# A planned one-core kernel of chunked attention and a gated convolution layer: a new order of all steps, new choices of engines, another rule for filler matmuls

## The chip, the cores and the metric

The kernel runs on one core of a Trainium2 chip. The metric is the device time of one execution in microseconds. A run is one execution; the time before is the median of three.

## What is computed

```python
scores = scale * np.matmul(q_c, k_c.transpose(0, 1, 2, 4, 3))   # chunks of 64 rows, 8 x 8 x 9 of them
scores = scores - np.max(scores, axis=-1, keepdims=True)
attn = np.exp(scores)
attn = attn / (np.sum(attn, axis=-1, keepdims=True) + 1e-09)
out = np.matmul(attn, v_c)                                      # B, H, S, D = 8, 8, 576, 64
x = np.ascontiguousarray(attn_out.transpose(0, 2, 1, 3)).reshape(B, S, H * D)
...
h = np.maximum(x @ w_in, 0.0)                                   # 512 -> 1024
for k in range(K):                                              # 3 taps along the sequence
    conv_out += conv_w[k][None, None, :] * hp[:, k:k + S, :]
gate = 1.0 / (1.0 + np.exp(-conv_out))
return (h * gate @ w_out).astype(np.float32)                    # 1024 -> 512
```

The three weights arrive as 64-bit floats. The kernel reads them as pairs of 32-bit words and turns each into a high and a low part itself.

## The kernel before

**Tiles.** The 4608 rows of q, k and v are 36 tiles of 128 rows (two chunks of 64), numbered t0 to t35. Tiles t0 to t8 load their rows straight into one of three slots (`load_rows`, lines 126 and 133) and TensorE (PE) transposes them (`t_pe`, lines 196 and 201); t9 and later come by way of DRAM (`shuffle`, line 151; `load_part`, line 169) and VectorE (DVE) transposes them (line 217). Then come the scores (line 247, 32 matmuls), the maximum (line 257), the difference (261), the exponential on ScalarE (ACT, line 266), the sum (270), the small value added to it (274 or 276), the reciprocal (279) and the normalisation (line 319, on GpSimd, POOL, or DVE). PE transposes the probabilities (line 326), ACT or DVE copies them (lines 76 and 78), and `attn_v` multiplies them with the values (line 339, 32 matmuls). `x_hi` (ACT, line 394) and `x_lo` (DVE, line 398) put the result as two parts into the input of the next layer. From t12 on two tiles share a step `both` (the scores of two tiles and the values' product of the two before them; twelve such steps have scores), and their probabilities go through `s_fold`, `s_scale` and `p_swap`: two passes on POOL or DVE, then four small DMAs of SyncE's queue (line 313), then a transpose on DVE.

**First product.** The 4608 columns are twelve units u of 384. A block `mm1` (line 408) is one unit and one of eight groups of 128 features: 12 matmuls. Behind it ACT and DVE apply the rectifier (416, 418), the taps (446, 451), the tanh (462) and the gate (481).

**Second product.** It works on pairs of row tiles with seven products of 12 matmuls (`product`, line 512) in place of eight. Its factors are made from the gated values: a cast (lines 76, 78), a remainder (499), sums and differences (502). `product` needs all parts of w_out.

**Weights.** w_in is loaded in six pieces (two halves each of its first two quarters, then two quarters), w_out in four, conv_w in one, through `w_load` (line 544), into two places `w0` and `w1`. Each piece is taken apart: a scaled copy on ACT (558), a shift (562) and a word step (567) on DVE, a cast to the high part (76, 78), the remainder (571). For w_out the sums of Strassen's scheme come after the word step: differences on POOL (589 to 591), low parts (584 and 597). The piece of w_out loaded last is its second one. conv_w has small steps of its own on DVE (601 to 635). When the last word step and the last transpose of direct rows are done (`slot_users`), the memory of the slots is given to the ring of later tiles and to the factors of the second product.

**The order.** Nothing above runs in the order of the program text. Each call of `step` (line 80) notes an operation with an engine, a length and what it must follow; there are 1873, numbered in the order of the calls. `moved_` (line 963) puts some on another of their engines: entry x moves step x // 4 to its choice x % 4. `order_` (line 991) lists all steps. A loop goes through it, gives each step the earliest start that its engine, its predecessors and its buffers allow in a simple model of the machine, and hands out buffers. Then (line 1136) the steps are emitted by planned start, and a fixed order on each engine is kept. All DMAs are issued from SyncE's queue (SP) in that order, and one that has to wait holds those behind it.

**Fillers.** Up to a planned 110 us, line 1140 puts transposes of the identity matrix into planned gaps of PE:

```python
pe_free, until_ = 2.0, 110.0
...
            for _ in range(int((begin[i] - pe_free) / 0.14) if idle else 0):
                nc.tensor.transpose(out=banks[idle[-1]][:, 0:P], in_=ident, identity=ident)
            pe_free = begin[i] + steps[i]["cost"]
```

## Time and profile before

| | us |
|---|---|
| median of 3 runs | 478.6 (476.5 to 479.18) |
| the profiled execution | 477.3 |
| its span, from the first to the last instruction | 475.5 |
| PE, DVE, ACT, POOL busy | 464.0, 413.0, 257.7, 289.4 |
| first block of line 408 starts | 39.75 |
| first product of line 512 starts | 87.46 |

The page's busy shares are means over the span. Matmuls are pipelined and their ends are modelled, so PE can be busy throughout a stretch in which it does little, and a filler counts as busy like any other matmul. The order of time and the stretches tell the stages apart.

### The profile page before, as it was taken

Reading aid. Unit: us, or ns where it says so; the run is one execution under the profiler, and the core shown is the slowest. Engines: PE = TensorE matmul, PEld = TensorE weight load, DVE = VectorE, ACT = ScalarE, POOL = GpSimd, SP = SyncE. Lnnn points to the kernel's source line nnn. Section 1 sums busy time; section 2 is a strip of 40 time slices with the busy share of each in tenths; the row PEclk is TensorE's granted clock in tenths of the full one; section 3 lists DMA queues with packets and bytes.
Section 4 is the critical chain, followed back from the end, with each engine's and each line's share of the span. In section 5 each row is a group of like instructions: output and inputs, shape, how many; then the busy total and the mean of one; then the engine's idle time right before and its main releaser. Section 6 shows DMA issues by size and latency. Waiting matters only on the chain.

```text
span 475.5 us, 13438 instructions
## 1 busy us (share of the span) xinstructions
PE 464.0 (98%) x5481; PEld 452.9 (95%) x5481; DVE 413.0 (87%) x775; ACT 257.7 (54%) x535; POOL 289.4 (61%) x260
## 2 busy tenths in 40 slices
PE   8989889999999999999999999999999999999996
PEld 8879889999999999999999999999999999999996
DVE  2869999999999898989988999898998998788694
ACT  2557989955555463554564465453545545444631
POOL 0124678976777666767667857467868553633523
PEclk9989999999999999999999999999999999999999
DMA  6878999998789999999938283600361100101002
GB/s 195 237 216 255 282 207 193 188 162 205 133 143 211 200 204 160 157 228 165 221 80 149 60 208 80 166 23 23 102 167 45 46 23 2 46 1 68 8 38 112
DMA packets 186369, 64.33 MB, mean 135 GB/s; under 512 B 159660, under 2 KB 177092, under 8 KB 186308
## 3 DMA queue, kind: packets, MB, share of 16 engines
q1 hardware_dynamic: 186308, 63.48, 61.9%
q8 instruction: 43, 0.70, 0.6%
q14 instruction: 18, 0.15, 0.1%
HBM read 50.88 MB, written 23.59 MB: 157 GB/s over the span
## 4 chain that ended last, share of the span: by engine, by line
PE 89%; DVE 5%; ACT 2%; issue 2%; POOL 1%; POOLq 0%; DVEq 0%
PE b_ps L512 38%; PE b_ps L408 38%; PE sx_ps L247 3%; PE sx_ps L339 3%; PE b_ps L196 2%; PE b_ps L1140 2%; PE z_ps L339 1%; DVE wt L567 1%; PE z_ps L247 1%; PE b_ps L326 1%; DVE gt L451 1%; DVE wt L562 1%; DVE m L257 1%; ACT wt L558 0%; DVE wt L261 0%
## 5 line engine op out<-in xcount | busy, mean ns | idle before, releaser
L512 PE MATMUL b_ps<-wo_h,f 128*128 128x256 f32 x1008 | 190.6, 282 | 0.1
L512 PEld LDWEIGHTS b_ps<-wo_h,f 128*128 128x128 f32 x1008 | 158.6, 188 | 2.2 <-POOL f L78 0.7
L512 PE MATMUL b_ps<-wo_l,f 128*128 128x256 f32 x504 | 141.3, 280 | 0.6 <-issue 0.6
L451 DVE SCALAR_TENSOR_TENSOR gt<-b_ps,cw,gt 128x384 f32<-128x384 f32 (+3 forms) x208 | 116.6, 576 | 9.0 <-ACT gt L446 7.1
L499 POOL TENSOR_TENSOR f<-gt,f 128x512 fp32r<-128x512 f32 x71 | 91.8, 1298 | 29.3 <-ACT f L76 9.8
L512 PEld LDWEIGHTS b_ps<-wo_l,f 128*128 128x128 f32 x504 | 94.9, 188 | 0.3 <-issue 0.3
L408 PE MATMUL b_ps<-x_h,wi_h 128*128 128x386 f32 (+2 forms) x384 | 84.7, 342 | 0.9 <-DVE gb L481 0.9
L408 PE MATMUL b_ps<-x_l,wi_h 128*128 128x386 f32 (+2 forms) x384 | 83.3, 338 | 0.0
L408 PE MATMUL b_ps<-x_h,wi_l 128*128 128x386 f32 (+2 forms) x384 | 83.1, 338 | 0.0
L462 ACT ACTIVATE gt<-gt 128x384 f32<-128x384 f32 (+2 forms) x96 | 50.2, 523 | 43.8 <-DVE gt L451 43.6
L408 PEld LDWEIGHTS b_ps<-x_l,wi_h 128*128 128x128 f32 x384 | 68.8, 188 | 0.0
L408 PEld LDWEIGHTS b_ps<-x_h,wi_l 128*128 128x128 f32 x384 | 68.6, 188 | 0.0
L408 PEld LDWEIGHTS b_ps<-x_h,wi_h 128*128 128x128 f32 x384 | 65.7, 188 | 1.8 <-DVE gb L481 1.2
L446 ACT ACTIVATE gt<-b_ps,cw 128x384 f32<-128x384 f32 (+2 forms) x104 | 56.4, 555 | 18.0 <-DVE b_ps L418 16.3
L416 ACT ACTIVATE b_ps<-b_ps 128x386 f32<-128x386 f32 (+2 forms) x78 | 37.3, 479 | 51.5 <-PE b_ps L408 47.6
L502 POOL TENSOR_TENSOR gt<-gt 128x512 f32<-128x512 f32 x43 | 55.5, 1295 | 15.2 <-PE b_ps L408 6.0
L481 DVE SCALAR_TENSOR_TENSOR gt<-gt,b_ps 128x192 f32<-128x192 f32 (+2 forms) x120 | 47.2, 410 | 8.1 <-ACT gt L462 7.4
L78 POOL CAST f<-gt 128x512 fp32r<-128x512 f32 x42 | 25.8, 613 | 33.9 <-PE b_ps L512 24.1
L76 ACT CAST f<-gt 128x512 fp32r<-128x512 f32 x43 | 26.5, 617 | 25.2 <-PE b_ps L512 14.8
L217 DVE STREAM_TRANSPOSE qkT<-qk 128x1024 f32<-128x1024 f32 (+1 forms) x30 | 33.3, 1119 | 0.4 <-DMA qk<-rows 0.4
L524 ACT ACTIVATE wt<-b_ps 128x256 f32<-128x256 f32 x50 | 18.9, 381 | 24.9 <-PE b_ps L512 24.9
L499 POOL TENSOR_TENSOR f<-gb,f 128x512 fp32r<-128x512 f32 x14 | 18.1, 1294 | 17.8 <-ACT f L76 8.7
(96 smaller groups left out, 614.8 us busy)
## 6 DMA issues: line engine op xcount, KB each, us to landing
out<-wt SPq DMA_DIRECT2D x36, 256.0 KB, 3.7
qk<-rows SPq DMA_DIRECT2D x24, 320.0 KB, 5.0
rows<-in_k SPq DMA_DIRECT2D x12, 576.0 KB, 8.7
rows<-in_q SPq DMA_DIRECT2D x12, 576.0 KB, 8.3
qk<-rows SPq DMA_DIRECT2D x24, 256.0 KB, 4.5
v<-in_v SPq DMA_DIRECT2D x21, 256.0 KB, 5.0
w<-in_moe_w_out SPq DMA_DIRECT2D x4, 1024.0 KB, 6.1
wt<-wt SPq DMA_DIRECT2D x48, 64.0 KB, 2.0
```

The costliest lines, as they stand in the source:

```text
L76: nc.scalar.copy(out=out, in_=in_)
L78: ENG[eng].tensor_copy(out=out, in_=in_)
L217: nc.vector.transpose(out=to[:, :, i:i + n], in_=of[:, :, o:o + n])
L408: nc.tensor.matmul(h_ps[:, 0:w], lhsT=wt[:, f // 2, kt, P * (f % 2):P * (f % 2) + P], rhs=xt[:, u % NX, kt, 0:w], start=n == 0, stop=n == ...
L416: nc.scalar.activation(out=h, in_=h, func=AF.Relu)
L446: nc.scalar.mul(out=g, in_=h, mul=cw[:, FT + f:FT + f + 1])
L451: nc.vector.scalar_tensor_tensor(out=g, in0=h, scalar=w, in1=g, op0=ALU.mult, op1=ALU.add)
L462: nc.scalar.activation(out=g, in_=g, func=AF.Tanh, scale=0.5)
L481: nc.vector.scalar_tensor_tensor(out=o, in0=g, scalar=1.0, in1=hv, op0=ALU.add, op1=ALU.mult)
L499: ENG[eng].tensor_tensor(out=part(st, 1), in0=quarter(*src), in1=part(st, 0).bitcast(F32), op=ALU.subtract)
L502: ENG[eng].tensor_tensor(out=quarter(*out_), in0=quarter(*a), in1=quarter(*b), op=op)
L512: nc.tensor.matmul(o, lhsT=part(ft, a)[:, j, :], rhs=w[:, i, j, :], start=first and n == 0, stop=n == 3 * FT // 2 - 1, skip_group_check=True)
```

## The change

The diff touches what a reader can put into four groups.

1. Options that are set to nothing: `PLAIN = 0` (a second product without Strassen's scheme for the first pairs), `TAPS = 0` (the convolution's taps as matmuls for the first units), `HOMED = ()` (rows loaded into the place of the gated values). Their functions and branches are in the text and emit nothing. The step numbers stay the same, 0 to 1872.
2. The model of loads: other lengths (`lag`), a limit of eight outstanding DMAs in the queue, a limit on how far the queue runs ahead (`ahead`), and a count of DMAs in a step (`m`). They act on planned starts alone.
3. Both lists, `moved_` (197 entries before, 194 after, 80 in both) and `order_`, are new.
4. The rule for fillers.

```diff
-            ld = step("SP", 1.2 if (2 * t) % NCK < NCK - 1 else 2.3, load_key, load_rows, (st, t), take=[(r, st)], lag=1.9 if t < NP else 2.8)
+            cost = 1.2 if (2 * t) % NCK < NCK - 1 else 2.3
+            ld = step("SP", cost, load_key, load_rows, (st, t), take=[] if t in HOMED else [(r, st)], lag=(2.35 if cost < 2 else 2.9) if t < NP else 3.0,
+                      ahead=1.7 if t < NP else 1.1, m=2 if cost < 2 else 4)
...
-    dma_free, kind, bank = 3.5, 0, {}
+    dma_free, ring_end, kind, bank = 1.6, {"SP": 0.0, "ACT": 0.0, "POOL": 0.0}, 0, {}
+    landed = {"SP": [0.0] * 8, "POOL": [0.0] * 8}
...
-        if e == "SP":
-            dma_free = max(dma_free, t + 0.3 + cost / 2) + s["lag"]
-            end[i] = max(dma_free + 1.5, t + cost + 2.0)
         free_at[e] = t + cost - early[e]
+        if s["lag"]:
+            ring, x = landed["SP" if e == "ACT" else e], t
+            for j in range(s["m"]):
+                x = max(x, ring[-8 + j]) + cost / s["m"]
+            free_at[e] = max(x, ring_end[e]) - early[e]
+            dma_free = max(dma_free, x - cost / 2 + 0.3) + s["lag"]
+            end[i] = max(dma_free + 1.5, x + 2.0)
+            ring += [end[i] - s["lag"] * (s["m"] - 1 - j) / s["m"] for j in range(s["m"])]
+            ring_end[e] = dma_free - s["ahead"]
...
-    pe_free, until_ = 2.0, 110.0
+    pe_free, until_ = 1.4, 110.0
...
-            for _ in range(int((begin[i] - pe_free) / 0.14) if idle else 0):
+            wait = begin[i] - pe_free - 0.3
+            for _ in range(int((wait + 0.3) / 0.164) if pe_free < 2.0 else int(wait / 0.115) + 1 if idle and wait > 0 else 0):
                 nc.tensor.transpose(out=banks[idle[-1]][:, 0:P], in_=ident, identity=ident)
```

What the numbers of the two lists mean, for the parts that the prediction speaks of (wi0a is the first half of the first quarter of w_in, wo1 the second piece of w_out, rows, v, and so on with their tile):

```
SP, before:  rows t0, cw, rows t1, rows t2, wi0b, rows t3, wi0a, v t0, rows t4, wi1a, rows t5, v t1, wi1b, wi3, v t2, ...
SP, after:   rows t0, rows t1, wi0a, cw, rows t2, v t0, rows t3, wi0b, rows t4, wi1a, v t1, wi1b, rows t5, v t2, wi3, ...
             (wo1 is the 27th load in both)

PE, before:  ... t_pe t3 (2), scores t2, p_pe t0, t_pe t4 (2), attn_v t0, p_pe t1, scores t3, t_pe t5, scores t4, attn_v t1, ...
             attn_v t2, p_pe t3, t_pe t6 (2), mm1 u0
PE, after:   ... scores t2, t_pe t3 (2), p_pe t0, attn_v t0, scores t3, t_pe t4, p_pe t1, t_pe t4, attn_v t1, p_pe t2, scores t4, ...
             attn_v t2, scores t5, p_pe t3, mm1 u0
   ahead of the first product, before alone: one mm1 block of u1; after alone: attn_v t7

DVE, after, of what stood ahead of the last word step (wo1) from the copy of t0's second half on:
   no longer there: copies of q and k of t1 (2) and t5, the normalisation of t4, the remainder of wi1a
   new there:       six steps of cw (they ran before that copy), the cast of wi0a, the remainder of wi0b, the copies of the
                    probabilities of t2 and t3, a copy of q and k of t6, the normalisations of t3 and t6, three small softmax steps
   of it ahead of the start of mm1 u0: all new ones but the copies of t3 and t6, the normalisation of t6 and two of the
                    small steps; and the shift and word step of wi3 and the maximum of t5 stand behind it now

POOL, before: ... differences wo2, low parts wo2 (2), differences wo1, f_sum, normalisation t7, low part wo1, last low part wo1
POOL, after:  ... differences wo2, low part wo2, differences wo1, low part wo1, last low part wo2, last low part wo1, f_sum
   of 12 s_fold and 12 s_scale: 9 and 12 on POOL before, 11 and 11 after; 241 steps on POOL before, 228 after
```

## Rows read from the trace of the kernel before

**Rows 1.** The page: busy time, share of the span and number of instructions of PE, PE's weight loads, DVE, ACT and POOL.

```profile
PE 464.0 (98%) x5481; PEld 452.9 (95%) x5481; DVE 413.0 (87%) x775; ACT 257.7 (54%) x535; POOL 289.4 (61%) x260
```

**Rows 2.** Busy time by stretch: the stretch and its length, then busy us of each engine (with the number of instructions), the granted PE clock, the DMA engines' busy share and GB/s.

```profile
9.57:24.73 15.16, 13.77 (x375) 11.82 (x376) 12.50 (x24) 6.75 (x13) 1.89 (x2) 1.00 0.82 221
24.73:28.70 3.97, 3.55 (x65) 2.98 (x65) 0.00 (x1) 2.63 (x6) 0.94 (x1) 0.58 0.66 181
28.70:39.75 11.05, 10.32 (x197) 9.49 (x196) 10.48 (x19) 6.71 (x15) 3.57 (x6) 1.00 0.82 249
39.75:87.46 47.71, 44.47 (x467) 42.31 (x464) 46.23 (x98) 43.52 (x89) 33.65 (x30) 1.00 1.07 234
...
39.75:87.46 47.71, 2.37 (x17) 1.76 (x15) 1.00 1.07 234
...
110.00:471.50 361.50, 360.74 (x3981) 356.59 (x3980) 321.34 (x579) 182.19 (x380) 230.32 (x201) 1.00 0.53 111
```

The shorter row for 39.75 to 87.46 is the same view of the fillers (line 1140) alone.

**Rows 3.** The waits of PE over the whole span: who waited for whom, us in total, times, the longest.

```profile
PE sx_ps L339 <- ACT p_all L76: 1.5, 1, 1.5
...
PE b_ps L408 <- DVE gb L481: 0.9, 1, 0.9
PE b_ps L512 <- issue: 0.6, 1, 0.6
```

**Rows 4.** The fillers (line 1140): duration in ns (least, median, most), first and last start; and the sum of their busy time over the seven stretches of 10 us that hold any, on PE and of the weight loads.

```profile
L1140 PE MATMUL b_ps<-ident x112: 271/273/472, 1.4 to 93.7; 128*128 128x128 f32 x112
...
sum 70.00, PE 18.43 PEld 14.63; mean PE 2.63 PEld 2.09
```

**Rows 5.** PE in order of time: start, us, line, operation, out<-in, count, and in brackets the idle time before it with its releaser.

```profile
1.36 5.73 PE L1140 MATMUL b_ps<-ident 128*128 128x128 f32 x35 [1.36 <-POOL ident masks.py:199]
7.02 1.16 PE L196 MATMUL b_ps<-ident,qk 128*64 128x64 f32 x32
...
25.15 0.88 PE L339 MATMUL sx_ps<-p_all,v 64*64 64x64 f32 x26 [1.81 <-issue]
...
27.43 1.13 PE L247 MATMUL sx_ps<-qkT 64*64 64x64 f32 x32
...
30.26 0.69 PE L247 MATMUL sx_ps<-qkT 64*64 64x64 f32 x32
...
39.75 0.95 PE L408 MATMUL b_ps<-x_h,wi_h 128*128 128x384 f32 x4
...
87.46 0.36 PE L512 MATMUL b_ps<-wo_h,f 128*128 128x256 f32 x1
```

**Rows 6.** The waits of DVE from 0 to 90 us, columns as in rows 3.

```profile
DVE m L257 <- PE sx_ps L247: 5.9, 3, 4.0
```

**Rows 7.** The waits of SP's queue over the whole span, columns as in rows 3.

```profile
SPq L313 <- POOL wt L307: 53.9, 8, 18.4
...
SPq L126 <- PE b_ps L196: 2.9, 1, 2.9
```

**Rows 8.** Line 126 between 0.6 and 2.2 us, its first two DMAs: duration of the issue, and the time from issue to landing.

```profile
L126 SPq DMA_DIRECT2D qk<-in_q x1: 767/767/767, 0.7 to 0.7; - x1
L126 SPq DMA_DIRECT2D qk<-in_k x1: 635/635/635, 1.6 to 1.6; - x1
...
DMA to landing us min/median/max: 3.3/3.4/3.4
```

**Rows 9.** The page's DMA queues (packets, MB, share of 16 engines' span) and its DMA issues (count, KB each, median us to landing).

```profile
q8 instruction: 43, 0.70, 0.6%
...
wt<-wt SPq DMA_DIRECT2D x48, 64.0 KB, 2.0
```

**Rows 10.** DVE and POOL in order of time, columns as in rows 5.

```profile
22.39 0.68 DVE L567 SCALAR_TENSOR_TENSOR wt<-w,wt 128x512 uint32<-128x512 uint32 x1
22.99 0.68 DVE L270 TENSOR_REDUCE z<-wt 128x8 f32<-128x512 f32 x1
...
72.38 2.05 DVE L567 SCALAR_TENSOR_TENSOR wt<-w,wt 128x1024 uint32<-128x1024 uint32 x1
...
74.57 2.39 POOL L597 TENSOR_TENSOR wo_l<-wt,wo_h 128x1024 fp32r<-128x1024 f32 x1 [1.23 <-ACT wt L266]
77.66 1.28 POOL L589 TENSOR_TENSOR wt<-wt 128x512 f32<-128x512 f32 x1 [0.69 <-DVE f L499]
...
79.84 0.74 POOL L591 TENSOR_TENSOR wt<-wt 128x256 f32<-128x256 f32 x1
...
82.79 2.02 POOL L584 TENSOR_TENSOR wo_l<-wt,wo_h 128x256 fp32r<-128x256 f32 x2
84.76 2.45 POOL L597 TENSOR_TENSOR wo_l<-wt,wo_h 128x1024 fp32r<-128x1024 f32 x1
```

**Rows 11.** Groups of instructions on DVE: out<-in, shapes, count | busy us, mean ns of one | idle us before them.

```profile
L78 DVE COPY qkT<-b_ps 128x512 f32<-128x512 f32 x5 | 3.3, 677 | 1.7 <-PE b_ps L196 1.7
...
L614 DVE SCALAR_TENSOR_TENSOR wt<-w,wt 24x128 f32<-24x128 uint32 x1 | 0.3, 278 | 0.0
L610 DVE TENSOR_SCALAR wt<-w 24x128 uint32<-24x128 uint32 x1 | 0.2, 207 | 0.0
```

**Rows 12.** The chain of work in order of time: start, us, what.

```profile
107.76 2.11 PE b_ps L408 x12
...
114.54 0.62 PE sx_ps L339 x32
```

More of the change, by code (lines that the diff above doesn't have):

```diff
@@ L58, in attn_ffn @@
     DIRECT = ()
+    PLAIN = 0
+    TAPS = 0
+    HOMED = ()
     scale = 1.0 / float(D) ** 0.5
@@ L71, in attn_ffn @@
     steps = []
-    ENG = {"DVE": nc.vector, "POOL": nc.gpsimd}
+    ENG = {"DVE": nc.vector, "POOL": nc.gpsimd, "SP": nc.sync, "ACT": nc.scalar}
     def copy_on(eng, out, in_):
@@ L78, in copy_on, with step @@
             ENG[eng].tensor_copy(out=out, in_=in_)
-    def step(eng, cost, key, fn, args=(), after=(), take=(), free=(), lag=0.0, port=False, bank=None, other=(), soft=()):
+    def step(eng, cost, key, fn, args=(), after=(), take=(), free=(), lag=0.0, port=False, bank=None, other=(), soft=(), ahead=1.1, m=1):
         s = dict(eng=eng, cost=cost, key=key, fn=fn, args=args, after=[a for a in after if a], take=take, free=free,
-                 lag=lag, port=port, bank=bank, other=other, soft=[a for a in soft if a])
+                 lag=lag, port=port, bank=bank, other=other, soft=[a for a in soft if a], ahead=ahead, m=m)
         steps.append(s)
@@ L678, in split_o @@
         st = {}
-        ld = step("SP", 0.55, t_load, w_load, (st, src_o[n]), take=[("wslot", st)], lag=3.5)
+        ld = step("SP", 0.55, t_load, w_load, (st, src_o[n]), take=[("wslot", st)], lag=3.5, ahead=5.0)
         s1 = step("ACT", 1.15, key, w_scale, (st,), [ld], take=["wt"])
@@ L819, in ring @@
                         shuffled[b, i] = [step("SP", 0.55, key - 20 + 0.1 * n, shuffle, (b, i, n), lag=4.0) for n in range(2)]
-                    got += [step("SP", 0.55, key + 0.1 * n, load_part, (c0, c1, i, n), slot_users + old + shuffled[b, i], lag=1.35) for n in range(2)]
+                    got += [step("SP", 0.55, key + 0.1 * n, load_part, (c0, c1, i, n), slot_users + old + shuffled[b, i], lag=1.45, ahead=3.0) for n in range(2)]
                 group_loads.update(dict.fromkeys(range(c0, c1), got))
@@ L888, in pair_steps, with mul, copy @@
         w_all = [x for n in range(FT // 2) for x in wo_done[n]]
-        def mul(name, i, key, bank_, half, first, after, take=()):
+        def mul(name, i, key, bank_, half, first, after, take=(), free=(("ft", "ft"),)):
             ft = fts[name]
             before["o"] = step("PE", 1.425, key, product, (st, ft, i, bank_, half, first), [ft["made"]] + w_all + after,
-                               take=list(take), free=[("ft", "ft")], soft=[before.get("o")])
+                               take=list(take), free=list(free), soft=[before.get("o")])
             return before["o"]
-        def copy(row, col, key, after, **kw):
-            return step("ACT", 0.39, key, o_copy, (st, row, col), after, other=[("DVE", 0.43, False)], **kw)
+        def copy(row, col, key, after, bank_="y", **kw):
+            return step("ACT", 0.39, key, o_copy, (st, row, col, bank_), after, other=[("DVE", 0.43, False)], **kw)
+        if p < PLAIN:
+            for row, b_ in enumerate("yq"):
+                at = key + 4 + 4 * d * row
+                one, two = f"A{row + 1}1", f"A{row + 1}2"
+                x = mul(one, 0, at, b_, 0, True, [], [("bk", st, b_)], [])
+                c = copy(row, 1, at, [x, before["st"] if row else None], b_, **({} if row else {"take": ["wt"]}))
+                if not row:
+                    before["st"] = c
+                x = mul(two, 1, at + d, b_, 0, False, [c], [], [])
+                c = copy(row, 0, at + d, [x, c], b_)
+                x = mul(one, 3, at + 2 * d, b_, 1, True, [c])
+                x = mul(two, 2, at + 3 * d, b_, 1, False, [x])
+                e = step("DVE", 0.43, at + 3 * d, o_last, (st, row, 1, b_), [x, c], free=[("bk", b_)])
+                last = step("SP", 0.5, key + 13 + row / 2, o_store, (st, 2 * p + row), [e, c] + ([last] if row else []),
+                            free=["wt"] if row else [], lag=0.65, ahead=5.0)
+            return
         p1 = mul("A11", 0, key + 4, "y", 0, True, [], [("bk", st, "y")])
@@ L927, in wi @@
             end for i, ks in enumerate(parts)
[L928 removed]
+            for end in split(key + 2 * i, t_load + 0.1 * i, src_i[n][:, ks], wi_h[:, n, ks, :], wi_l[:, n, ks, :], half=len(parts) > 1,
+                             at=None, **kw)]
     cw_done = split(8.0, 0.15, src_c)
@@ L953, in attn_ffn @@
             pair_steps(3 * (u - 1) // 2 + 2, PK[3 * (u - 1) // 2 + 2])
+    for s, f in home_next:
+        s["after"] += [home_users[i] for i in range(len(home_users)) if 1024 * i < 2 * UN * (f + 1) and 1024 * (i + 1) > 2 * UN * f]
     for s, over in x_writes:
```

133 lines of the change are left out of this document (89 added, 44 removed), and 212 rows, old and new, of tables (moved_, order_).

## The prediction

> **What bounds the kernel now.** I read the page first: TensorE (PE) is busy 98% of the span, VectorE (DVE) 87% [rows 1]. A share over the whole span hides stages, so the next view was busy time by stretch [rows 2]. From 110 to 471.5 us PE is busy 360.74 of 361.5 us, and of the waits that its list names only the "issue" of 0.6 us lies there [rows 3]: nothing is left to gain in that stage, whose matmuls are the same in both kernels. The last fourteen PE steps stand in the same order in both lists, so the end is the same too. So a gain has to come from before 110 us, where PE is "busy" partly with fillers: 112 of them cover 18.4 us [rows 4], and only 2.4 us of that lies between 39.75 and 87.46 [rows 2].
>
> What holds PE there? The first block of the first product (line 408) starts at 39.75 us, the first of the second (line 512) at 87.46 [rows 5]. Between them DVE is busy 46.23 of 47.71 us, ACT 43.52, PE 44.47 with fillers [rows 2]: this stretch is DVE's. Before it DVE loses time: 2.66 us in 9.57 to 24.73, and then 3.97 us in one piece (24.73 to 28.70), a wait for the scores of tile 3 [rows 2, 6]. The cause stands in PE's order of time: the attention product of tile 0 stopped after 6 of its 32 matmuls and went on with 26 at 25.15; the 1.81 us ahead of them are "issue", no wait that the profile shows. [...]
>
> The load queue (SP) has a hole as well: the rows of tile 3 wait 2.9 us for the slot that tile 0's transposes still read, and all loads behind them with it [rows 7].
>
> **The change part by part.** The new options (PLAIN, TAPS, HOMED) are zero or empty, so no new instruction runs. Live are the order, 194 engine choices (80 of the 197 old ones stay), the rule for fillers, and the plan's model of loads, which acts through the other three alone.
>
> *First fillers.* The old rule puts (6.94 - 2.0)/0.14 = 35 of them ahead of the first transposes; the row has 35, from 1.36 to 7.02, that is 0.162 us each [rows 5]. The two loads which those transposes read were issued at 0.7 and 1.6 us and landed 3.4 and 3.3 us later [rows 8], by 4.9: the fillers, not the data, held the start back. By the new lines of the loop (1.6 in place of 3.5 for the queue's start, lag 2.35 for 1.9) the planned start is 5.49, so (5.49 - 1.4)/0.164 = 24 fillers; these are counts that the code emits. 11 x 0.162 = 1.8 us, less 0.1 for a wait on the data: **-1.7** at the start of every chain; the slot comes free as much earlier. Bounds: 0 (data late) and -2.1 (7.02 - 4.9). Later fillers: planned gaps up to 0.3 us get none now (up to two before), gaps of 0.5 us two in place of three, gaps over 1 us the same or one more. One filler takes 0.27 us [rows 4], in a gap that mostly waits anyway; I take 0 and put -0.5 into the range.
>
> *The stall at 23 us.* In the new lists tile 0's values are loaded ahead of tile 3's rows, where the hole in the queue was, and on PE the scores of tile 3 come right behind the attention product of tile 0, with tile 4's transposes behind them in place of in front. DVE has weight work and softmax of tiles 1 and 2 to do ahead of those scores. If the stall goes, DVE keeps its 3.97 us; if it comes back at the same count of PE instructions, it hits the transposes of tile 4, which no engine needs soon. I take **-4.0**; bounds 0 (it returns on the path) and -4.0.
>
> The queue table has 43 packets of the instruction queue, 0.70 MB [rows 9], 16 KB each. [...]
>
> *DVE's work.* I counted, in both lists, the DVE steps from its copy of tile 0's second half (9.57 us) to the last weight piece's word step (line 567, ends at 74.43 [rows 10]); all factors of the second product wait for that one, since their buffers lie where the weight slots were. Out: three copies of q and k to ACT, a normalisation and a weight remainder to POOL, 5 steps of 0.68 us. In: six small steps on the convolution weights that ran ahead of 9.57 (1.48 us together), a weight cast, a remainder, two copies of probabilities, one of q and k, two normalisations (0.68 each), and 1.05 us of small softmax steps (one sum as long as a copy, a reciprocal, the small value added) [rows 11]. That is 7.29 - 3.40 = 3.9 us; consecutive DVE steps overlap by 0.08 us (22.39 + 0.68 against 22.99 [rows 10]), for 11 more steps 0.9: **+3.0** on the path. Its bounds are 0 (other work stands in PE's way) and +3.9. For the start of line 408 the same count gives 1.8 us less DVE work than before, so that start should come at 39.75 - 1.7 - 4.0 - 1.8 = 32.2, at the latest 36.
>
> *The chain behind it on POOL.* Before: word step done at 74.43, the difference on POOL from 77.66, then a sum and a normalisation, low parts of 2.02 and 2.45 us, end 87.21 [rows 10], product at 87.46 [rows 5]: 12.8 us on POOL's side. Now the difference comes ahead of the other piece's remainder (2.39), and sum and normalisation are behind it or on DVE: from 77.66 on without the two in between, that is 2.9 (77.66 to 80.58) + 2.0 + 2.4 + 2.45 = 9.8 us. **-3.0**; bounds -3.0 and 0 (if the shared order of DVE and POOL holds the difference back as before).
>
> *PE's order.* One block of line 408 (2.11 us) moved behind the first product, one attention product (0.62) ahead of it [rows 12]: **+1.5** still to do at that point. Changes between kinds of matmuls are as many, within two.
>
> *Everything later:* 0. Its covers are the 40 us that DVE and the 131 us that POOL are idle from 110 us on [rows 2]; if they fail, PE waits: third rival.
>
> **Sum:** -1.7 - 4.0 + 3.0 - 3.0 + 1.5 = -4.2 us at the first product, kept to the end since PE is full from there. The profiled execution took 477.3 us (span 475.5), so 473.1; the median of the runs is 1.3 higher, 478.6, so **474.4 us**, -0.9%. About 0.5% (2.4 us) is what a measurement of this kernel can tell from no change.
>
> **Rivals.** (1) The stall returns on the path: the -4.0 falls away, the sum is -0.2, **478.4 us**. For: the wait belongs to no data, and PE runs through as many instructions in the first 30 us as before. Against: the new order puts nothing urgent there. (2) DVE doesn't set the first product, PE's own work does. Then the start's gain is kept whole (1.7 + 4.0 + 1.8, less 0.9 for two transposes that moved behind it, 6.6), and of the 3.2 us of idle time and 2.4 us of fillers between 39.75 and 87.46 [rows 2] half goes too: -9.4, **469.2 us**. Against: DVE's 97% in that stretch. (3) Slower: the twelve combined steps of tiles 12 on wait for probabilities that pass POOL, four DMAs of 2.0 us to landing [rows 9] and DVE; SP, in order, already waits 53.9 us for POOL ahead of those DMAs, once 18.4 [rows 7]. The new lists give POOL 22 of their 24 folding and scaling passes in place of 21, and put stores and loads of values elsewhere in SP's order. From (4.2 + 2.4)/12 = 0.55 us of lateness at each step the kernel would be slower by over 0.5%; at 0.6 us it is +7.2 - 4.2, **481.6 us**. Against: that wait doesn't once reach PE now [rows 3], and POOL has 13 steps fewer. (4) Fewer fillers drop the clock. A fall like the one at 25 us costs half of its stretch of 4 us, so three among line 408's blocks would undo the gain and give again about 478. Idle pieces of 0.9 and 1.5 us [rows 3] left the clock at 1.00 from 28.70 on [rows 2], so this is counted inside (1).
>
> [...]
>
> **How the numbers follow.** Forecast 0.48, its own range 471.8 to 477.4 (-0.5 and -2.1 at the fillers on one side; POOL's 3.0 lost on the other). Rivals 1 and 4: 0.25; rival 2: 0.13; rival 3: 0.14. Faster by over 0.5%: the forecast without its upper edge, and rival 2: 0.60. Within 0.5%: rival 1 and that edge, 0.26. Slower: 0.14. The range 470.5 to 479.4 leaves out rival 3 and half of rival 2.
>
> **What would show it.** Right: first transposes at about 5.3 us behind some 24 fillers; no DVE wait near 4 us for the scores of tile 3; line 408 from 32 to 36 us; first product at about 82; the last remainder (line 597) ends right ahead of it. Wrong: an "issue" wait of over 1 us on PE with scores behind it (rival 1); PE waiting for POOL or DVE between 75 and 90 us (the -3.0); PE waiting for probabilities or x in the combined steps (rival 3); a granted clock under 1.00 after 35 us (rival 4).

## The result and the profile after

The changed kernel takes 482.58 us (median of 8 runs, 480.59 to 484.92), the kernel before 478.08 in the same session (8 runs, 476.5 to 483.43). The ratio is 1.0109 with a 95% interval of 1.0086 to 1.0132: slower by 1.1%, where 474.4 was forecast. The profiled execution took 480.59 us, 3.3 more than that of before, with a span of 478.8. Line numbers have moved: 408 is 414 now, 512 is 549, 247 is 253, 339 is 345, 196 is 202, 1140 is 1227. Runs with a disturbed clock are left out of all comparisons.

The page, answering [rows 1]. Every engine but ACT has less to do:

```profile
PE 463.4 (97%) x5477; PEld 452.5 (95%) x5477; DVE 409.3 (85%) x773; ACT 265.5 (55%) x550; POOL 277.4 (58%) x247
```

The waits of PE over the whole span, answering [rows 3]:

```profile
PE b_ps L549 <- issue: 2.0, 1, 2.0
PE sx_ps L345 <- ACT gt L483: 1.8, 1, 1.8
PE b_ps L207 <- DVE gb L518: 1.4, 1, 1.4
...
PE b_ps L202 <- DMA qk<-in_k: 1.2, 1, 1.2
...
PE z_ps L253 <- issue: 0.7, 1, 0.7
```

PE in order of time, answering [rows 5]:

```profile
1.36 4.58 PE L1227 MATMUL b_ps<-ident 128*128 128x128 f32 x24 [1.36 <-POOL ident masks.py:199]
5.86 2.10 PE L202 MATMUL b_ps<-ident,qk 128*64 128x64 f32 x64
...
9.43 1.16 PE L202 MATMUL b_ps<-ident,qk 128*64 128x64 f32 x32 [1.22 <-DMA qk<-in_k]
10.52 0.70 PE L253 MATMUL sx_ps<-qkT 64*64 64x64 f32 x32
...
21.99 0.69 PE L345 MATMUL sx_ps<-p_all,v 64*64 64x64 f32 x32
22.51 0.65 PE L253 MATMUL sx_ps<-qkT 64*64 64x64 f32 x32
...
35.93 0.94 PE L414 MATMUL b_ps<-x_h,wi_h 128*128 128x384 f32 x4
...
66.08 0.91 PE L345 MATMUL sx_ps<-p_all,v 64*64 64x64 f32 x32 [1.80 <-ACT gt L483]
...
69.92 0.96 PE L414 MATMUL b_ps<-x_h,wi_h 128*128 128x388 f32 x4
...
86.93 0.28 PE L549 MATMUL b_ps<-wo_h,f 128*128 128x256 f32 x1
...
162.74 1.16 PE L345 MATMUL sx_ps<-p_all,v 64*64 64x64 f32 x64
163.72 1.11 PE L253 MATMUL z_ps<-qkT 64*64 64x64 f32 x64
...
169.04 0.51 PE L549 MATMUL b_ps<-wo_h,f 128*128 128x256 f32 x2 [2.02 <-issue]
...
211.28 0.34 PE L253 MATMUL z_ps<-qkT 64*64 64x64 f32 x8 [0.68 <-issue]
```

A wait for "issue" is one for which the trace shows nothing that PE waited for; it is called an issue wait below, and unit 1 begins with the first matmul of 388 columns. Read from the top: 24 fillers, transposes at 5.86 (7.02 before). The attention product of tile 0 runs through at 21.99 and the scores of tile 3 follow at once: the stall of 23 us is gone. Line 414 starts 3.8 us earlier than line 408 did. But unit 1 (69.92 against 67.97) is 1.9 us later, the first product only 0.5 us earlier, and behind it two waits for "issue" come to 2.7 us where before had 0.6.

So 3.3 us are made up of -0.5 at the first product and +3.8 behind it (478.8 - 86.93 = 391.9 us, before 388.0). Of the 3.8, 1.5 are the PE order that the prediction counted and 2.1 the issue waits. The medians lie 4.5 us apart, 1.2 more than the profiles: the runs of after have a mean granted clock of 0.993 (0.988 to 0.996, the profiled one 0.996), 16 runs of before in the next session 0.9985. A straight line through after's eight runs gives 3.3 us more for each 0.01 of clock lost (correlation 0.81), so the clock would account for the 1.2; that is a fit, not an experiment.

### The profile page after: what moved, and what is told of

Read it like the earlier page. It is cut to its first block, busy times and chain, and to the rows that moved or that the text cites. A ratio compares the mean times of both kernels' runs of the same rounds, so it can differ in the third digit from the quotient of the medians.

```text
span 478.8 us, 13446 instructions
## 1 busy us (share of the span) xinstructions
PE 463.4 (97%) x5477; PEld 452.5 (95%) x5477; DVE 409.3 (85%) x773; ACT 265.5 (55%) x550; POOL 277.4 (58%) x247
## 4 chain that ended last, share of the span: by engine, by line
PE 88%; DVE 5%; DMA 2%; ACT 2%; issue 1%; POOL 1%; SPq 0%; ACTq 0%; POOLq 0%; DVEq 0%
PE b_ps L414 40%; PE b_ps L549 38%; PE sx_ps L345 2%; PE sx_ps L253 2%; PE z_ps L345 1%; DMA qk<-in_k 1%; PE b_ps L202 1%; PE z_ps L253 1%; DVE wt L605 1%; DMA w<-in_moe_w_in 1%; PE b_ps L1227 1%; ACT wt L596 1%; POOL wi_l L609 1%; DVE x_l L404 1%; PE b_ps L332 0%
## 5 line engine op out<-in xcount | busy, mean ns | idle before, releaser
L536 POOL TENSOR_TENSOR f<-gt,f 128x512 fp32r<-128x512 f32 x61 | 79.0, 1299 | 47.3 <-ACT f L79 22.1
L539 POOL TENSOR_TENSOR gt<-gt 128x512 f32<-128x512 f32 x41 | 52.9, 1293 | 11.2 <-DVE f L536 5.3
L79 ACT CAST f<-gt 128x512 fp32r<-128x512 f32 x50 | 30.8, 617 | 30.5 <-PE b_ps L549 26.0
L81 POOL CAST f<-gt 128x512 fp32r<-128x512 f32 x36 | 22.0, 612 | 35.7 <-PE b_ps L549 21.9
L561 ACT ACTIVATE wt<-b_ps 128x256 f32<-128x256 f32 x55 | 20.6, 381 | 22.3 <-PE b_ps L549 22.3
L536 POOL TENSOR_TENSOR f<-gb,f 128x512 fp32r<-128x512 f32 x18 | 23.3, 1294 | 16.5 <-ACT f L79 9.2
```

The costliest lines, as they stand in the source:

```text
L79: nc.scalar.copy(out=out, in_=in_)
L81: ENG[eng].tensor_copy(out=out, in_=in_)
L536: ENG[eng].tensor_tensor(out=part(st, 1), in0=quarter(*src), in1=part(st, 0).bitcast(F32), op=ALU.subtract)
L539: ENG[eng].tensor_tensor(out=quarter(*out_), in0=quarter(*a), in1=quarter(*b), op=op)
```

## Where the lead of 3.8 us goes

Busy time by stretch, columns as in [rows 2]: from the first scores to the first block of line 414 (408), and from there to the end of DVE's first piece of x_l of tile 6 (128x4), which unit 1's second four matmuls read. First after, then before, then e8, the old lists without the stall (below).

```profile
10.52:35.93 25.41, 24.16 (x608) 21.83 (x605) 21.37 (x47) 15.31 (x30) 4.47 (x5) 1.00 0.81 228
35.93:67.96 32.03, 26.84 (x329) 24.72 (x327) 30.40 (x55) 26.75 (x52) 17.97 (x18) 0.98 0.96 252
```

```profile
10.80:39.75 28.95, 26.41 (x607) 23.25 (x603) 22.11 (x41) 16.10 (x32) 6.40 (x8) 0.94 0.81 226
39.75:67.96 28.21, 25.45 (x330) 23.97 (x328) 27.07 (x49) 26.79 (x52) 16.48 (x15) 1.00 1.04 260
```

```profile
9.80:36.89 27.09, 24.96 (x607) 22.03 (x603) 22.18 (x41) 16.20 (x32) 6.61 (x8) 1.00 0.89 242
36.89:64.93 28.04, 25.75 (x331) 24.36 (x329) 26.57 (x49) 26.54 (x52) 16.21 (x14) 1.00 0.96 257
```

The third busy figure is DVE. Up to the first block after has 4.04 us of idle DVE (25.41 - 21.37), before 6.84, e8 4.91. In the second stretch after has 30.40 us of DVE work in 32.03, before 27.07 in 28.21: 3.3 us more, and the stretch is 3.8 us longer. It ends at 67.96 us in both kernels, so the lead of 3.8 us is gone there: the early start is owed work. After's unit 1 then begins another 1.95 us later than before's. e5 (below) has the same PE steps there, its x_l piece ends at 67.93, and its granted clock is 1.00 from 60 to 70 us, where after's is 0.83. First after, then e5:

```profile
66.92 1.11 PE L207 MATMUL b_ps<-ident,qk 128*128 128x128 f32 x4
67.83 2.34 PE L1227 MATMUL b_ps<-ident 128*128 128x128 f32 x11
```

```profile
66.68 0.66 PE L207 MATMUL b_ps<-ident,qk 128*128 128x128 f32 x4
67.17 1.36 PE L1232 MATMUL b_ps<-ident 128*128 128x128 f32 x11
68.29 0.95 PE L414 MATMUL b_ps<-x_h,wi_h 128*128 128x388 f32 x4
```

So in these two executions the clock costs after 1.6 us at unit 1 (69.92 against 68.29), of which 1.0 is in the eleven fillers that the new rule puts there (before has four). At the first product 0.8 is left (86.93 against 86.15).

## Experiments

A matmul takes two places in PE's program, itself and its weight load (the pages have as many of both, 5477 in after and 5481 in before), and each of the small matmuls below appears in the trace as two (e1's 73 as 146, e6's 40 as 80); the expectations count places, the text matmuls as the trace has them. Each kernel has 6 to 12 runs. Results are medians, with ratios to the kernel before in the same session (477.1 to 478.0 us) and their 95% intervals.

### Do the issue waits hang on the place in the program?

The expectations set two theories against each other. 'Blocks': an issue wait hangs on how many matmuls PE has run, so a shift takes it away or moves it. 'Place': it belongs to its time, whatever stands there, and stays. By 'blocks' e1 was expected at about 480 us, and e5, further below, at about 480.5 with under 1 us of issue waits behind 110 us.

**e1, e2.** In after and in before, nine of the first fillers become 73 small matmuls, so that everything behind stands 137 matmuls later.

```diff
-            for _ in range(<24 in after, 35 in before>):
+            for _ in range(73):
+                nc.tensor.matmul(banks[idle[-1]][0:64, 0:64], lhsT=ident[0:64, 0:64], rhs=ident[0:64, 0:64], start=True, stop=True)
+            for _ in range(<15, 26>):
```

> The changed kernel with 9 of its 24 first fillers replaced by 73 small ones (64x64), so that every later PE instruction stands 128 places further in PE's instruction stream. [...] Rival 'place': the waits belong to what else the chip does at 167 and 210 us, not to the count of instructions. Then they stay and the time is 482.6.

> The kernel before with the same shift of 128 places (9 of its 35 first fillers replaced by 73 small ones). Theory 'blocks': the issue wait of 0.6 us near 165 us goes, and the one of 1.8 us at 23 us (row 962 of PE's instructions) leaves the attention product of tile 0; without it the stretch to line 408 is up to 4 us shorter, of which PE's later order keeps up to 2. About 475.5 to 477.5 in place of 478.1. Rival 'place': both stay, 478.1.

Measured: 500.62 us (1.0483, 1.0433 to 1.0533) and 493.13 (1.0319, 1.0275 to 1.0363). The times tell nothing of the issue waits, since the small matmuls were slow:

```profile
1.36 15.83 PE L1228 MATMUL b_ps<-ident 64*64 64x64 f32 x146 [1.36 <-POOL ident masks.py:199]
```

What holds is that the waits changed: behind 110 us e1 has 5.1 us of them (after 2.7) and e2 2.5 (before 0.6), and e2 has no early stall. Both expectations had the late waits go; they grew.

**e3, e4.** The program of after with both lists of before, and the program of before with both lists of after: the lists apart from the filler rule.

```diff
-    moved_, order_ = <the kernel's own lists>
+    moved_, order_ = <the other kernel's lists>
```

> The changed kernel's program (its model of loads and its rule for fillers) with both lists of the kernel before. If the lists carry the loss: 478 within 1, first filler gap of 24, line 408's first block near 39, the issue wait near 165 us as before. If the rule for fillers carries it: 481 to 483, with a granted clock under 1.00 between 35 and 110 us.

> The kernel before (its model and its rule for fillers, 119 fillers in all) with both new lists. If the lists carry the loss: 481 to 483; line 408's first block at 36 to 37, unit 1's first block near 70, 0.9 us behind in PE's work at 110 us. If the rule for fillers carries it: 478 within 1 and no fall of the clock at 66 us.

Measured: e3 480.15 us (1.0037, 1.0007 to 1.0068), line 414 at 39.99 behind three early issue waits of 0.8 to 1.2 us, first product 87.05, 2.7 us of issue waits behind it. e4 485.82 (1.0169, 1.0123 to 1.0214), line 408 at 35.68, 6.4 us of issue waits in five pieces. e3 lies between its two expected times, e4 above both of its own. So the lists decide when line 408 (414) starts, and the number of fillers ahead decides something that the plan's model doesn't hold: in later steps the matmuls stand 11 (e4) and 9 (e3) places further on than the same lists had them, and the issue waits grow by 3.7 and 2.1 us while the medians grow by 3.2 and 2.1. Two of e4's waits:

```profile
168.54 0.57 PE L512 MATMUL b_ps<-wo_l,f 128*128 128x256 f32 x1 [2.37 <-issue]
...
190.43 0.80 PE L408 MATMUL b_ps<-x_h,wi_h 128*128 128x388 f32 x3 [1.47 <-issue]
```

The number of matmuls that PE has run shows what they share. Busy time from the start to each wait, after (two waits), before (the early stall and its late wait) and e4 (those two):

```profile
0.00:166.90 166.90, 157.79 (x2250) 150.26 (x2250) 144.79 (x293) 106.68 (x221) 96.67 (x93) 0.99 0.94 202
0.00:211.00 211.00, 199.48 (x2757) 190.90 (x2758) 183.94 (x365) 129.12 (x268) 126.48 (x117) 0.99 0.94 193
```

```profile
0.00:24.50 24.50, 21.99 (x475) 19.61 (x476) 14.37 (x31) 8.64 (x16) 2.69 (x9) 1.00 0.77 213
0.00:165.60 165.60, 158.38 (x2250) 150.31 (x2251) 143.29 (x288) 107.20 (x222) 98.77 (x95) 0.99 0.95 202
```

```profile
0.00:168.00 168.00, 158.38 (x2251) 150.47 (x2251) 145.91 (x294) 106.17 (x220) 96.64 (x93) 0.99 0.94 202
0.00:190.00 190.00, 178.80 (x2505) 170.32 (x2505) 162.56 (x320) 116.81 (x243) 108.74 (x103) 0.98 0.92 192
```

475, 2250, 2251, 2505 and 2757 are multiples of 127 plus 90 to 94. In after, before and e1 to e15 every issue wait over 0.3 us stands at a remainder of 87 to 95. And 127 matmuls are about what comes to one packet of the instruction queue: 43 packets [rows 9] for 5477 or 5481 matmuls, 127.4 each. The 127 matmuls from one such count to the next are called a block here. The packets of that queue in after's 166.5 to 167.0 us, and in before's 22.6 to 22.8 (after has none from 163.1 to 166.5, before none from 21 to 22.6):

```profile
q8 instruction: 1, 0.02, 13.2%
```

```profile
q8 instruction: 1, 0.02, 28.9%
```

In after the block that ends at matmul 2250 begins in the middle of the step at 162.74, whose 128 small matmuls run in 2.1 us; PE was through with the block in 3.9 us (163.0 to 166.9). The packet turned up in the last half microsecond of that, and PE went on at 169.04. The trace doesn't say which block a packet holds, but the times agree: in four of these waits (two each in after and before) a packet starts at 166.6, 208.6, 22.7 and 163.7 us, and PE goes on 2.4 to 2.7 us later, at 169.04, 211.28, 25.15 and 166.17. Before's late wait is the short one (0.58 us), with a packet that starts 1.7 us into the block; in after's long one (2.02) it starts 3.5 us into it. A block full of line 414's matmuls lasts by estimate 127 x 0.176 = 22 us (12 in 2.11 [rows 12]), long beside those 2.4 to 2.7 us.

**e5, e6.** If the place decides, a shift by half a block (64 matmuls) should part the combined steps from the block ends. The small matmuls now rotate over four corners and two banks.

```diff
+            for n_quad in range(<38 in after, 40 in before>):
+                a_, z_ = 64 * (n_quad % 2), 64 * (n_quad // 2 % 2)
+                nc.tensor.matmul(banks[idle[-1 - n_quad % 2]][z_:z_ + 64, 64 * (n_quad // 4 % 8):64 * (n_quad // 4 % 8) + 64],
+                                 lhsT=ident[a_:a_ + 64, a_:a_ + 64], rhs=ident[a_:a_ + 64, a_:a_ + 64], start=True, stop=True)
-            for _ in range(<24, 35>):
+            for _ in range(<12, 19>):
```

> The changed kernel with 12 of its 24 first fillers replaced by 38 small matmuls in four quadrants (two rows each, of some 0.02 us as in the scores), so that all later PE instructions stand 128 places further on in its stream, half a block, and the first transposes start at 6 to 7 us. [...] Rival 'place': 482.6 or, with the later start, up to 484.

> The kernel before with 16 of its 35 first fillers replaced by 40 small matmuls in four quadrants, 128 places further on likewise. Theory 'blocks': the issue wait near 165 us (0.6) goes and none over 0.3 comes after 110 us, and the early one of 1.8 us leaves the attention product of tile 0: 476 to 477.5 in place of 478. Rival 'place': 478 to 479.

Measured: e5 481.32 us (1.0089, 1.0052 to 1.0125), issue waits 1.6 in place of 2.7. e6 475.41 (12 runs; 0.9947, 0.9921 to 0.9972): no issue wait behind 110 us, one of 1.6 at 27 and two of 0.3 and 0.4 ahead of it. **e6 is faster than both kernels.** Where its 0.5% comes from isn't shown in full: in the profiles its first product comes 0.65 us earlier than before's, and the rest lasts as long (388.1 us, before 388.0), with a wait of 1.2 us for DVE in a combined step where the issue wait had been. e5's 1.6 us is above the 1 that was expected, and its profiled execution is the fastest of its runs, 2.4 us under the median. Issue waits behind 110 us by shift, all kernels but e13 (1.3) and e14 (0.8):

| shift in matmuls | old lists | new lists |
|---|---|---|
| -16 | | 3.1 (e7) |
| -12 | 0 (e8), 1.4 (e12) | |
| 0 | 0.6 (before) | 2.7 (after) |
| +9 to +11 | 2.7 (e3), 2.5 (e2) | 5.1 (e1), 6.4 (e4) |
| +63 to +65 | 0 (e6, e11, e16) | 1.6 (e5), 2.9 (e9), 1.5 (e10), 0.8 (e15) |

The place has a large part in it, but not all: e8 and e12, or e5 and e9, have the same counts and waits of other lengths; why isn't shown.

### What are the first fillers worth?

**e7, e8, e9.** After with 8 first fillers; before with 23; and e5 with the rows of tile 2 loaded ahead of the first piece of w_in (in `order_`, with that piece's scale and shift moved to right ahead of its word step).

```diff
-            for _ in range(<24 in after, 35 in before>):
+            for _ in range(<8, 23>):
```

> The changed kernel with 8 first fillers in place of 24: all later PE instructions 32 places earlier in the stream. Theory 'blocks': shifts of +18 and +22 places made the issue waits grow, so one of -32 makes them shrink: under 1.5 us after 110 us, about 481 in place of 482.6. Rival 'place': no change in them. On the front both say: the first transposes start at 5.0 us, when tile 0's rows have landed, and those of tile 1 still at 9.4, with its rows, so nothing of it is kept, unless the clock of the first stretch falls.

> The kernel before with 23 first fillers in place of 35: the term of the prediction for them (-1.7 us) by itself, and all later PE instructions 24 places earlier in the stream. As predicted: line 408 1.7 us earlier. Rival 'rows of tile 1': these land at 9.36 us, so the second pair of transposes starts at 9.4 to 9.7 as before and line 408 moves by under 0.4 us. Theory 'blocks' adds: the issue wait near 165 us under 0.6; total 477 to 478.5.

> The kernel of e5 (new lists, shifted by 128 places, the same counts of fillers) with the load of tile 2's rows ahead of the first piece of w_in instead of behind it, and that piece's scale and shift right ahead of its word step. Theory 'loads': tile 1's rows share the DMA engines with that piece and land at 9.1 to 9.3 us; now they land by 8, the scores of tile 0 start by 9.2 in place of 10.2, and 1 us of it reaches line 408 (34.9 in place of 35.9) and the first block of unit 1. Rival: the piece lands 2 us later, its shift and word step hold DVE, and line 408 comes no earlier or up to 2 us later.

Measured: e7 483.35 us (1.0115, 1.0086 to 1.0144): its transposes start at 5.38, wait for data, take 3.68 us for the 64 that take 2.10 in after, and issue waits stay at 3.1, where a smaller sum was expected. e9 481.36 (1.0080, 1.0053 to 1.0105): first scores at 8.98, but line 414 only at 37.02, so earlier rows alone don't speed the start (34.9 was expected). e8 476.25 (0.9973, 0.9947 to 0.9999), with no issue wait anywhere and no stall:

```profile
9.80 0.69 PE L247 MATMUL sx_ps<-qkT 64*64 64x64 f32 x32
...
36.89 0.94 PE L408 MATMUL b_ps<-x_h,wi_h 128*128 128x384 f32 x4
...
84.42 0.36 PE L512 MATMUL b_ps<-wo_h,f 128*128 128x256 f32 x1
```

In the old order 12 fillers fewer bring 1.0 us at the first scores (10.80 before), and with the stall gone 2.9 at line 408 and 3.0 at the first product. There the lead is kept up to the first product; in after it isn't. But e8's profiled execution is the fastest of its runs, 2.7 us under their median, and before's (477.3) is at the median of that session (477.35): in the medians 1.1 us of it is left.

### Is it DVE's work?

**e10, e12.** Five steps that the new lists gave to DVE (copies of the probabilities of t2 and t3, a copy of q and k of t6, the normalisations of t3 and t6): e10 takes them from DVE in e5, e12 puts them on DVE in e8.

```diff
-    moved_: ... 549, ... 977, 985, ... 1169, ... 1205 ...      (e10: taken out of e5; e12: put into e8)
```

> The kernel of e5 with five steps given back to the engines they had in the kernel before: the copies of the probabilities of tiles 2 and 3 and a copy of tile 6 to ACT, the normalisations of tiles 3 and 6 to POOL (0.68 us each on DVE, three of them behind the start of line 408). Theory 'DVE owes': from the start of line 408 to the end of the remainder of x of tile 6 the new lists take 32.6 us, the old ones 28.1, since DVE has more to do there; this falls by about 2, to 30.6, and unit 1 starts by up to 3 us earlier. Rival 'ACT and POOL': they are as full and in an order made for the other choice; it stays at 32 to 33.

> The kernel of e8 (old lists, 23 first fillers) with the five steps of e10 put on DVE: the copies of the probabilities of tiles 2 and 3 and of a half of tile 6 from ACT, the normalisations of tiles 3 and 6 from POOL, 3.4 us of DVE work. Theory 'DVE owes': DVE is busy 48.75 of the 55.13 us from the scores of tile 0 to the end of the remainder of x of tile 6 in e8 and 52.37 of 58.04 in the changed kernel, so those 55.1 us grow by 2.5 to 3.5 and unit 1 starts at 67.5 to 68.5 in place of 64.9; the time is 2 to 3 us above e8. Rival 'order': DVE's idle 6.4 us there take the added steps in, the stretch grows by under 1 us, and it is the new order of the steps, not their count, that costs.

Measured: e12 479.69 us (1.0056, 1.0028 to 1.0084; e8 0.9973). Against e8 unit 1 is 1.96 us later, the last word step 2.5, the first product 2.45:

```profile
66.89 0.96 PE L408 MATMUL b_ps<-x_h,wi_h 128*128 128x388 f32 x4
...
86.87 0.36 PE L512 MATMUL b_ps<-wo_h,f 128*128 128x256 f32 x1
```

Five steps (3.4 us of DVE) undo most of what the 12 fillers and the stall had brought. (1.4 us of issue waits came back too, so its whole time is not DVE's alone.) e10: 482.13 us (1.0094, 1.0051 to 1.0137), no gain over e5. Its second stretch, and the step ahead of the attention product of t6:

```profile
36.80:70.34 33.54, 28.09 (x329) 25.07 (x328) 29.11 (x50) 27.56 (x54) 21.51 (x20) 0.94 0.93 238
...
66.52 1.12 PE L332 MATMUL b_ps<-ident,wt 128*128 128x128 f32 x4 [1.40 <-POOL wt L325]
```

DVE has 1.3 us less work there than in e5 (30.41), but the stretch is 1.5 us longer (33.54, e5 32.07), and POOL, which took two normalisations, has 21.51 in place of 17.98. PE now waits 1.4 us for one of them, the normalisation of t6, at 66.52, where e5's transposes ran at 63.60; the clock there is lower too (0.94, e5 1.00), and e10's profile has an early issue wait of 2.5 us at 12.6 that e5's hasn't. So adding the work to the old order costs what the theory says, and taking it from the new order gives nothing: there POOL is late in DVE's place. With the lower clock and the early wait beside it, e10 is no clean test of DVE's load.

### Which half of the lists costs it?

**e13, e14.** The lists cut at the first product: old in front and new behind, and the reverse. **e11.** The old lists with both shifts: 23 first fillers, and 48 small matmuls in place of the 20 fillers ahead of the scores of t5.

```diff
-    order_ = <one list>
+    order_ = <one list up to the first product> + <the other behind it>, moved_ likewise      (e13, e14)
-            for _ in range(<20 ahead of the scores of t5>):
+            for n_quad in range(48): <as in e6>                                                (e11)
```

> The kernel before with 23 first fillers (as e8, 24 places earlier until 29 us) and 48 small matmuls in four quadrants in place of the 20 fillers ahead of the scores of tile 5, so that everything later stands 128 places further on than in the kernel before. Theory 'blocks': both gains hold, line 408 near 37 without an early stall and no issue wait over 0.5 us after 110 us: 473 to 475.5, faster than every kernel so far. Rival 'place': as e8, 476 to 477.

> The old lists up to the first product and the new ones for all steps behind it, 128 places further on as e6 and e5. If the new lists lose only in front of the first product (and by issue waits): as e6, 475 to 476.5. If the rest of the new lists loses by itself: up to as e5, 479 to 481.5.

> The new lists up to the first product and the old ones for all steps behind it, 128 places further on. If the front carries the loss: as e5 less what issue waits e5 has, 479 to 481. If the rest carries it: as e6, 475 to 476.5.

Measured: e14 482.52 us (1.0093, 1.0052 to 1.0134), all of e5's 1.0089, so the new front alone costs as much as both halves together. The cut isn't clean: one block of line 414 (2.1 us) more stands ahead of e14's first product than of e5's. e13 478.64 (1.0029, 1.0005 to 1.0054) is slower than e6 (0.9947), but its first product comes only at 88.29, behind waits of PE for POOL at the cut itself, so what the new rest costs by itself stays open. e11 477.03 (0.9997, 0.9974 to 1.0021): no late issue waits, but an early stall came back (1.3 + 0.4 + 0.3), line 408 at 38.66. It was expected to beat e6 and didn't.

### What do fewer fillers do to the clock?

**e15, e16.** e5 with 13 fillers, meant for the wait ahead of the attention product of t6, and 6 more; e6 without the 15 fillers between 62 and 68 us (4, 7, 4). Both keep the place of all that follows within 2 matmuls, e16 by 48 small matmuls in place of e6's 40 at the start.

```diff
+            for _ in range(<13 ahead of attn_v t6, 6 ahead of the fifth block>): nc.tensor.transpose(...)      (e15)
-            for _ in range(<4, 7, 4>): nc.tensor.transpose(...)                                                 (e16)
```

> The kernel of e5 with 13 more fillers in the wait of 1.8 us ahead of the attention product of tile 6 (written into the place which that product overwrites) and 6 ahead of the fifth block of line 408, shifted to the same place in PE's stream behind them. Theory 'clock': the wait of 1.8 us near 64 us is what lets the clock fall in the runs; with it filled the mean granted clock of the runs rises from 0.995 to 0.998 or more and the median falls from 481.3 to about 480. Rival 'work': the clock stays where it is, and the time within 0.7 us of e5's.

> The kernel of e6 without the 15 fillers near 62 to 68 us (4, 7 and 4), at the same place in PE's stream behind them. Theory 'clock': the mean granted clock of the runs falls from 0.999 to 0.996 or less, as in the kernels with the new lists, and the time rises by 1 to 2 us over e6's 475.4. Rival: clock and time as e6, since the idle pieces there (1.5 us and less) left the clock at 1.00 before.

Measured: e16 477.36 us (0.9999, 0.9980 to 1.0018), 2 us behind e6; e15 481.60 (1.0083, 1.0051 to 1.0116), like e5. The stretch from 60 to 70 us, in after, e6 and e16, and e15's fillers:

```profile
60.00:70.00 10.00, 7.30 (x128) 6.53 (x126) 9.81 (x21) 8.59 (x19) 6.18 (x9) 0.83 1.09 214
```

```profile
60.00:70.00 10.00, 8.50 (x114) 7.80 (x114) 10.00 (x18) 9.37 (x19) 6.46 (x6) 1.00 1.10 213
```

```profile
60.00:70.00 10.00, 7.71 (x95) 7.05 (x96) 10.00 (x19) 8.67 (x18) 6.47 (x7) 0.83 1.02 162
```

```profile
68.58 1.64 PE L1231 MATMUL sx_ps<-ident 128*128 128x128 f32 x13 [1.75 <-DVE x_l L404]
```

In e16 PE waits where the fillers were, and the granted clock is 0.83, against 1.00 in e6. The runs of e16 have a mean clock of 0.9969 (e6 0.9992), those of e15 0.9978 (e5 0.9953). So the fillers go with a higher clock, and in the old order with up to 2 us. How much of the 2 us is theirs isn't shown: e16's first transposes start 1.0 us later (7.24, e6 6.25), and its profiled execution, the fastest of its runs, is 1.3 us shorter than e6's with the lower clock. Nor do waits alone settle the clock: after and e5 wait alike from 60 to 70 us (PE busy 7.30 in both), at 0.83 and 1.00.

e15 doesn't part the clock from the work. Its 13 fillers write what x_l still reads, so they didn't fill the wait: they stood behind it (1.75 us) and held the attention product back by another 1.6 us. Its profile also has an early issue wait of 2.3 us at 13.3 that e5's hasn't. What a truly filled wait is worth in the new order is open.

### The marks of all kernels

| us | line 408/414 | unit 1 | last word step ends | first product | span |
|---|---|---|---|---|---|
| before | 39.75 | 67.97 | 74.4 | 87.46 | 475.5 |
| e8 | 36.89 | 64.93 | 71.4 | 84.42 | 471.8 |
| e6 | 39.18 | 67.32 | 73.8 | 86.81 | 474.9 |
| e16 | 37.69 | 66.06 | 72.2 | 85.94 | 473.6 |
| e12 | 36.29 | 66.89 | 73.9 | 86.87 | 477.5 |
| after | 35.93 | 69.92 | 74.7 | 86.93 | 478.8 |
| e5 | 35.86 | 68.29 | 74.6 | 86.15 | 477.1 |
| e15 | 38.49 | 72.39 | 78.3 | 89.77 | 479.9 |
| e14 | 35.41 | 70.56 | 75.7 | 90.12 | 477.5 |

Kernels with the new front start line 414 as early as any (e15, behind its early issue wait, apart) and still reach the first product only at 86.2 to 90.1 us; e8 does so at 84.4. After and e5 are at the good end, the profiled executions of both being the fastest of their runs.

## Why the prediction was wrong, by its steps

**First fillers, -1.7: mis-sized, -0.3 in after.** The count of 24 was right and the transposes started at 5.86. What stood behind was the data of tile 1. Its two DMAs, in line 132 from 2.8 to 3.2 us, and their times to landing:

```profile
L132 SPq DMA_DIRECT2D qk<-in_k x1: 635/635/635, 2.9 to 2.9; - x1
...
DMA to landing us min/median/max: 4.1/5.2/6.4
```

The second one took 6.4 us to land, where the DMAs of [rows 8] took 3.4, with a piece of w_in issued right behind it; in e9, with the rows of t2 there instead, the second tile's transposes start at 7.89 without a wait for data. In after they start at 9.43 and the first scores at 10.52 (10.80 before). In the old load order the same edit gives 1.0 (e8). The prediction gave the whole gain to "the start of every chain" from the first tile's two loads alone.

**The stall, -4.0: the mechanism right, the size not.** The stall went, as forecast. But the idle time that it had caused did not all turn into work: DVE idle ahead of line 414 fell by 2.8 us in after (6.84 to 4.04) and by 1.9 in e8. With 0.3 from the fillers and 0.7 of work put off (22.11 to 21.37; 1.8 was predicted) that is the 3.8 of 35.93 against 39.75. The forecast was 32.2, "at the latest 36".

**DVE's +3.0: held (+3.3).** It is made of -0.7 ahead of line 414 (-1.8 was predicted) and of what came behind: from line 414's start to the last word step's end it was 38.7 us against 34.7, +4.0 (4.8 follow from the prediction's 32.2 and 71.7). e12 shows it by itself: five of those steps cost 2.5. With a start 3.7 us later than forecast, the word step ended at 74.65 in place of 71.7, no earlier than before. The net of the terms up to there came to +0.2, where -2.7 was predicted. This is where the gain of the early part fell through.

**POOL's -3.0: -1.9, and off the path.** DVE and POOL in order of time, answering [rows 10]:

```profile
73.17 1.48 DVE L605 SCALAR_TENSOR_TENSOR wt<-w,wt 128x1024 uint32<-128x1024 uint32 x1
...
75.39 1.30 POOL L627 TENSOR_TENSOR wt<-wt 128x512 f32<-128x512 f32 x1 [1.83 <-DVE wt L325]
...
80.80 4.77 POOL L635 TENSOR_TENSOR wo_l<-wt,wo_h 128x1024 fp32r<-128x1024 f32 x2
```

From 74.65 to the last low part (85.57) it is 10.9 us in place of 12.8; the difference starts 0.7 us behind the word step, since DVE does a normalisation first. The product starts 1.36 us later, since PE, without a gap from 70 us on, still has blocks and transposes to run. That is rival 2's bound, without its gain: PE had fallen behind at 66 to 70 us, where it waited 1.8 us, four transposes and eleven fillers took 1.11 and 2.34 us (e5 0.66 and 1.36), and unit 1 began 1.6 us later than in e5, at a granted clock of 0.83. The prediction had put the later fillers at 0.

**PE's order, +1.5: held**, with 0.2 us left over in the sum behind the first product.

**Everything later, 0: the step that failed outright.** Its covers were idle DVE and POOL time, and the third rival looked for probabilities that come late. Neither happened: PE waits for no engine there. What it has there are issue waits, 2.7 us in place of 0.6, +2.1. The 0.6 stood in [rows 3] and the 43 packets in [rows 9]; the term of the stall asked whether such a wait returns "at the same count", and looked at the first 30 us only. e3 to e6 show that shifts of 9 to 64 matmuls in the first 110 us move such waits, add to them or take them away. After has 43 packets and two issue waits over 0.3 us; ahead of these two the block holds most of a combined step (from 162.74 and from 208.63 us).

**The clock (rival 4, folded into 1): it came**, at 60 to 70 us (0.83, before 1.00) and in the spread of the runs (0.993 against 0.9985). The fall near 25 us that the rival prices is the 0.58 of 24.73 to 28.70 [rows 2]; half of that stretch is an estimate from it. Against e5 it cost after 1.6 us at unit 1 and 0.8 at the first product, and by the fit above it would account for the 1.2 us between medians and profiles. It isn't all that holds the new front back: e5's profile, at 1.00, reaches unit 1 at 68.29, no earlier than before, and e8's at 64.93.

Together, in profiles: -0.5 at the first product where -5.7 was forecast, and +3.8 behind it where +1.5 was. Not shown: what delays the packet at matmul 2250 more in after than in before, how much the clock and how much DVE's work cost the runs with the new front (e15 was to part them and doesn't), whether the early issue waits of e10 and e15 are in the other runs of e5 too, and why the first product scatters by 4 us among these kernels.

## What to carry to other kernels

Where the bottleneck engine shows "issue" waits, count its instructions up to each: if the counts share a remainder (here 87 to 95 by 127, where 127.4 matmuls come to one packet of the instruction queue), moving some dummy instructions in or out ahead is an edit of its own (e6, with 64 matmuls more and an earlier start, gained 0.5%), and any change of order has to be timed at more than one shift. A gap that is closed early is only worth what the engine that paces the stretch behind it can use: follow its owed work to the next meeting point before booking the gain. And a filler has two sides: with it the clock around a wait can be higher (1.00 in e6 and 0.83 in e16 without, from 60 to 70 us), but where it stands behind the wait (e15, 1.64 us) or runs longer than it (after's eleven, 2.34 us) it holds back the work behind.

## What the runs showed of the hardware

The late issue waits of PE in after (2.02 us) and before (0.58) stand behind blocks of 127 matmuls that it ran fast: in after the block that began at 163.0 us was done at 166.9, and PE went on 6.0 us after its start; in before 162.0, 165.6 and 4.2 us. It went on 2.4 to 2.7 us after a packet of the instruction queue started (four waits). Small f32 matmuls of 64x64 in one corner and one bank took 0.108 us a row (e1, 146 in 15.83), rotating over corners and two banks 0.030 (e6, 80 in 2.41):

```profile
1.36 2.41 PE L1142 MATMUL b_ps<-ident 64*64 64x64 f32 x80 [1.36 <-POOL ident masks.py:199]
```

Which of the two, corner or bank, makes the difference wasn't tried.
